# Retention followed by a low-rank mixer MLP on one core: U, V and batch 1 loaded in another order, by other queues, in smaller pieces

## The chip, the cores and the metric

The kernel runs on one core of a Trainium2 chip. The metric is the device time of one execution in microseconds. The kernel before was run seven times: median 248.86 us, from 248.56 to 249.55. One further execution was profiled, and all durations and views below come from it.

## The reference

The first half is a retention layer with a decaying state for each head (4 batches, 8 heads, 768 positions, head size 64). Its output, with the heads side by side, is `x` (4 x 768 x 512). The second half mixes along the sequence with a low-rank product and then runs a two-layer MLP with a residual:

```python
state = gamma[None, :, None, None] * state + np.einsum('bhd,bhe->bhde', k[:, :, t], v[:, :, t])
y[:, :, t] = scale * np.einsum('bhd,bhde->bhe', q[:, :, t], state)
...
h = xt @ U @ V                                   # xt is x with sequence and features exchanged
u = x + h.transpose(0, 2, 1)
ch = np.maximum(u @ w_ch1, 0.0) @ w_ch2
return (u + ch).astype(np.float32)
```

U is 768 x 32, V is 32 x 768, `w_ch1` is 512 x 2048, `w_ch2` is 2048 x 512. Inputs and output are fp32 in HBM; the products are computed in bf16.

## The kernel before, in words

**Stages.** Retention is computed in chunks of 128 positions (six in a batch), as scores within a chunk plus a query against the state that is carried from chunk to chunk. Batch 0 has a path of its own (`cast_early`, `turn_early`, `score_early`, `state_early`, `mix_early`), with two chunks (256 positions) at a time, since nothing else can run yet. Then come the low-rank product of batch 0 (`proj`, the product with V4 at L670, and the turned x that is added to it in PSUM by `x_turn`), and from there on the MLP. The MLP of batch b is a list of pieces (`mlp_pieces`): 16 `up` pieces of 512 columns, 16 of 256 columns, and 24 `down` pieces (six output tiles of 128 rows, four pieces of four matmuls each). A piece of four 512-column matmuls has the cost 0.864 in that list, and a batch has 41.5 in all.

**Weaving.** `weave` puts the retention of batch b+1 between the MLP pieces of batch b. Each step has a mark, which is a share of the list's cost at which it is put into the program: `AT` gives the marks of `score4` and `mix4` of the six chunks, `LR` those of the low-rank part, and `turn_chunk` (two transposes on DVE) and `prep_chunk` (casts on POOL) stand a fixed part of a step before the score. The order is written out by hand; each engine works through its own instructions in that order.

**Who loads what.** SP issues all loads of q, k and v. For batch 0 these are blocks of 256 positions (L158, L154). For batches 1 to 3, `load_whole` (L111) loads k and q of a whole batch by four DMAs each, into tiles of 32-partition stripes, and `feed_more` (L130) loads natural chunks of v (and of k for batches 2 and 3). SP has nothing to wait for after batch 0, so batch 1 follows it at once. POOL issues the weights with a cast to bf16 in the DMA: a quarter of w1 (`load_w1(0)`), U, four copies of V, three more quarters of w1, and later four quarters of w2 (L262, L256, L259, L267). POOL also makes the casts `ki` and `qi` and the scaled `vd` of a chunk (L83, L85), and issues the stores of the output (L427). Each of its DMAs carries one of eight semaphores in turn, and waits until the DMA that had it before has landed.

**Buffers that matter here.** There is one tile each for k and q of a batch (`kin`, `qin`), so batch b+1 can be loaded only once POOL has cast the last chunk of batch b. MLP results go through three PSUM banks (`mlp`). The output tiles `o_sb` have three buffers, so the sum of output tile j+3 on DVE waits until the store of tile j has landed.

Of the kernel before, what the change touches and what calls it, by code (L numbers as in the profile page):

```python
# [9 lines left out]
fp32 = mybir.dt.float32  # L10
# [6 lines left out]
def kernel(  # L17
# [52 lines left out]
    def evac(eng, dst, src):  # L70
        if eng == "A":
            nc.scalar.activation(dst, src, AF.Copy)  # L72
        else:
            nc.vector.tensor_copy(out=dst, in_=src)
# [32 lines left out]
    def load_whole(nm, b):  # L107
        open_in(nm, b)
        src = {"q": q, "k": k}[nm][b]
        for hp in (0, 2, 1, 3):  # L110
# [3 lines left out]
                in_=src[ds(2 * hp, 2)].rearrange("h (c t j) d -> t (h c) (j d)",  # L114
                                                 c=NCK, t=32))

    def feed_more():
        while n_fed[0] < len(feed) and n_held[0] < RING:
            key, src = feed[n_fed[0]]
            if key[0] == "T" and n_cast[key[1] - 1] < 2 * NCK:  # L120
                return
            n_fed[0] += 1
            if key[0] == "T":
                load_whole("k", key[1])
                load_whole("q", key[1])
                continue
            n_held[0] += 1
            t = rin.tile([P, 512], fp32, tag="in", name=f"in_{n_fed[0]}")
            ready[key] = t
            nc.sync.dma_start(out=t.rearrange("p (h d) -> p h d", h=H), in_=src)  # L130
# [2 lines left out]
        n_held[0] -= 1  # L133
        return ready.pop(key)

    for b in range(1, B):
        feed.append((("T", b), None))
        for ci in range(NCK):
            if b > 1:
                feed_natural("k", b, ci)  # L140
            feed_natural("v", b, ci)
    NB = S // 256
    early = {}
# [108 lines left out]
            prep_natural("k", b, ci)  # L252
        prep_natural("v", b, ci)

    def load_u():
        nc.gpsimd.dma_start(out=Ub, in_=moe_U.rearrange("(j p) r -> p j r", p=P))  # L256

    def load_v(c):
        nc.gpsimd.dma_start(out=V4[ds(RK * c, RK)], in_=moe_V)  # L259

    def load_w1(mb):
        nc.gpsimd.dma_start(  # L262
            out=w1b[:, :, ts(mb, 512)],
            in_=moe_w_ch1[:, ts(mb, 512)].rearrange("(c p) n -> p c n", p=P))
# [164 lines left out]
    def mlp_pieces(b):  # L429
        gT = gtp.tile([P, NM, S], bf16, tag="gT", name=f"gT_{b}")  # L430
        pieces = []
        n = [0]

        def up(m, lo, sz):
            def f():
                g_p = bank("mlp")
                for c in range(NCB):
                    nc.tensor.matmul(g_p[:, :sz], w1b[:, c, ts(m, P)],  # L438
                                     uTs[b][:, c, ds(lo, sz)], start=(c == 0),
                                     stop=(c == NCB - 1))  # L440
# [12 lines left out]
        hold = {}  # L453

        def down(j, m0):
            def f():
                if m0 == 0:
                    hold[j] = bank("mlp")
                ch = hold[j]
                for m in range(m0, m0 + 4):  # L460
                    nc.tensor.matmul(ch, gT[:, m, ts(j, P)], w2b[:, m],  # L461
                                     start=(m == 0), stop=(m == NM - 1))
                if m0 == NM - 4:
                    o_sb = outp.tile([P, DM], fp32, tag="o_sb",
                                     name=f"o_{b}_{j}")
                    nc.vector.tensor_tensor(o_sb, ch, us[b][:, j], op=ALU.add)  # L466
                    stores.append((out[b, ts(j, P)], o_sb))
            return f

        for j in range(NCK):  # L470
            for m0 in range(0, NM, 4):
                pieces.append((0.864, down(j, m0)))
        return pieces
# [178 lines left out]
    def proj(js):  # L652
        for j in js:
            for c in range(NCB):
                nc.tensor.matmul(p_p[ds(RK * c, RK), :P], Ub[:, j],  # L655
                                 xs[0][:, j, ts(c, P)], start=(j == 0),
                                 stop=(j == NCK - 1))

    state_early(4)
    for c in range(NCB):  # L660
        x_turn(c, range(2))
    mix_early(2, "DA")
    proj(range(4))
    for c in range(NCB):
        x_turn(c, range(2, NLO))
    proj(range(4, NCK))
    pcs[0] = rmid.tile([P, P], bf16, tag="pc", name="pc_0")
    evac("D", pcs[0], p_p[:, :P])
    for c in (0, 2, 1, 3):
        nc.tensor.matmul(xT(c)[:, :LO], pcs[0][ds(RK * c, RK)],  # L670
                         V4[ds(RK * c, RK), :LO], start=False, stop=True,
                         skip_group_check=True)
# [12 lines left out]
    prep_natural("v", 1, 1)  # L685
    prep_natural("v", 1, 2)
    load_w2(2)
    load_w2(3)

    def at(b0, dc, dm):  # L690
        return [(b0 + dc * ci, b0 + dc * ci + dm) for ci in range(NCK)]

    AT = {1: at(0.36, 0.0625, 0.042), 2: at(0.09, 0.105, 0.05)}
    LR = {1: (0.80, 0.83, 0.88, 0.92), 2: (0.71, 0.75, 0.83, 0.89)}
    for b in range(1, B):
        w = min(b, 2)
        if b > 1:
            marks = [(0.02, part(lr_expand, b - 1, 4, 2)),
                     (0.06, part(lr_turn, b - 1, 4))]
        else:  # L700
            marks = [(0.03, part(lr_expand, 0, 4, 2)), (0.10, part(lr_turn, 0, 4)),
                     (0.16, part(lr_expand, 0, 0, 4))]
        step = AT[w][1][0] - AT[w][0][0]
        for ci in range(NCK):
            s_at, m_at = AT[w][ci]
            marks.append((s_at - 0.6 * step, part(turn_chunk, b, ci)))
            marks.append((s_at, part(score4, b, ci)))
            marks.append((m_at, part(mix4, b, ci)))
# [44 lines left out]
```

## Time and profile before

| what | value |
|---|---|
| median of seven runs | 248.86 us (248.56 to 249.55) |
| the profiled execution: its own time, its span | 249.43 us, 247.5 us |
| busy shares of the span: PE, DVE, ACT, POOL | 88%, 43%, 33%, 37% |
| first MLP matmul of batch 0, of batch 1 | 41.1 us, 97.4 us |
| last matmul starts, last store issued | 241.1 us, 242.5 us |
| moved by DMA in 247.5 us | 34.69 MB, mean 140 GB/s |
| DMA issued by SP (q1), by POOL (q0) | 23.60 MB, 10.73 MB |

The profiled execution took 0.57 us more than the median of the seven runs, and 1.93 us of its time lie outside the span. In the strips with 40 slices a slice is 6.2 us and a digit is a tenth: PE is busy with gaps in the first 45 us and then in nearly every slice to the end. The DMA strip is at 9 from the second slice to the sixteenth, that is to about 100 us, and from then on has holes.

### The profile page before, as it was taken

To read this page: it belongs to the slowest core of one execution; us is meant where nothing else is said; L and a number is where in the kernel's file an instruction comes from. 1 tells how busy PE (TensorE), PEld (TensorE's weight loads), DVE (VectorE), ACT (ScalarE), POOL (GpSimd) and SP (SyncE) were. 2 spreads that over 40 slices of the span, in tenths; PEclk is the share of its full clock that TensorE was granted. 3 is DMA by queue.
4 is the path that set the end of the run, shared out by engine and by line. 5 is a ranking of instruction groups with operands and counts; after the bars stand their busy time and mean duration, and the time that the engine had idled before them with its cause. 6 is when DMAs were issued, how large, how long until landed. Compare 5 with 4: busy or idle time off the path is not lost.

```text
span 247.5 us, 5673 instructions
## 1 busy us (share of the span) xinstructions
PE 217.7 (88%) x2412; PEld 119.9 (48%) x2412; DVE 106.4 (43%) x199; ACT 80.7 (33%) x176; POOL 90.9 (37%) x126
## 2 busy tenths in 40 slices
PE   1686607999999899899999999999999999999990
PEld 1465503447854444445754444457644444674440
DVE  4567104465555352466534525655545242322211
ACT  2474302535733104555641003555420024440000
POOL 2748540893602494851138516810011100001110
PEclk9996755899999999999999999999999999999998
DMA  6999999999799999129999853000012531001221
GB/s 186 290 294 208 226 225 197 201 181 199 157 203 203 217 259 250 43 74 209 211 192 256 213 144 98 16 3 4 0 45 87 128 106 21 3 0 42 86 86 42
DMA packets 63881, 34.69 MB, mean 140 GB/s; under 512 B 39664, under 2 KB 62320, under 8 KB 63856
## 3 DMA queue, kind: packets, MB, share of 16 engines
q1 hardware_dynamic: 56736, 23.60, 47.4%
q0 software_dynamic: 7120, 10.73, 18.3%
q8 instruction: 19, 0.31, 0.6%
q14 instruction: 6, 0.05, 0.1%
HBM read 30.90 MB, written 6.29 MB: 150 GB/s over the span
## 4 chain that ended last, share of the span: by engine, by line
PE 48%; issue 30%; DMA 9%; SPq 5%; POOL 3%; ACT 1%; DVE 1%; POOLq 0%; ACTq 0%
PE mlp L438 22%; PE mlp L461 17%; DMA Ub<-in_moe_U_dram 6%; DMA v<-in_v_dram 3%; SPq L158 3%; POOL out_dram L427 2%; SPq L154 2%; PE r L367 2%; PE r L334 2%; PE st L319 1%; PE r L358 1%; PE r L416 1%; ACT gT L445 1%; PE r L395 1%; PE mlp L296 0%
## 5 line engine op out<-in xcount | busy, mean ns | idle before, releaser
L438 PE MATMUL mlp<-uT,w1b 128*128 128x512 bf16 (+1 forms) x512 | 90.9, 330 | 2.4 <-ACT gT L445 1.2
L461 PE MATMUL mlp<-w2b,gT 128*128 128x512 bf16 x384 | 87.8, 379 | 1.1 <-issue 1.1
L445 ACT ACTIVATE gT<-mlp 128x512 bf16<-128x512 f32 (+1 forms) x88 | 42.7, 490 | 69.7 <-PE mlp L438 68.9
L438 PEld LDWEIGHTS <-w1b 128*128 128x128 bf16 x512 | 48.3, 98 | 35.2 <-issue 5.5
L461 PEld LDWEIGHTS <-gT 128*128 128x128 bf16 x384 | 35.8, 98 | 42.1 <-issue 1.8
L427 POOL DMA_DIRECT2D out_dram<-o x24 | 13.3, 556 | 94.3 <-DVE o L466 94.3
L443 DVE TENSOR_SCALAR gT<-mlp 128x512 bf16<-128x512 f32 (+1 forms) x40 | 22.1, 554 | 33.8 <-PE mlp L438 33.8
L466 DVE TENSOR_TENSOR o<-mlp,u 128x512 f32<-128x512 f32 x24 | 16.6, 690 | 42.8 <-PE mlp L461 42.8
L340 DVE TENSOR_TENSOR a<-r,mask 128x512 bf16<-128x512 f32 x36 | 23.2, 686 | 21.2 <-PE r L334 19.5
L85 POOL TENSOR_TENSOR qi<-qin,gqT 128x512 bf16<-128x512 f32 x18 | 18.8, 1046 | 22.0 <-DMA qin<-in_q_dram 15.1
L85 POOL TENSOR_TENSOR vd<-in,gk 128x512 bf16<-128x512 f32 x18 | 18.7, 1042 | 10.1 <-PE r L367 5.0
L72 ACT ACTIVATE x<-r 128x256 bf16<-128x256 f32 x36 | 11.8, 382 | 25.4 <-PE r L367 25.2
L402 DVE TENSOR_TENSOR u<-r,x 128x512 bf16<-128x512 f32 (+1 forms) x16 | 14.6, 951 | 4.2 <-PE r L395 4.2
L83 POOL CAST ki<-kin 128x512 bf16<-128x512 f32 x18 | 13.6, 766 | 7.6 <-DMA kin<-in_k_dram 5.0
L72 ACT ACTIVATE uT<-r 128x1024 bf16<-128x1024 f32 (+1 forms) x6 | 5.2, 880 | 21.8 <-PE r L670 11.3
L655 PE MATMUL mlp<-x,Ub 128*32 128x128 bf16 x24 | 1.0, 304 | 8.9 <-DMA Ub<-in_moe_U_dram 8.9
L83 POOL CAST kd<-in 128x512 bf16<-128x512 f32 x12 | 7.3, 610 | 1.6 <-POOL qi L85 1.6
L519 PE MATMUL mlp<-ident,kb 128*128 128x128 bf16 x24 | 3.1, 312 | 5.4 <-DVE kb L83 5.4
L284 DVE STREAM_TRANSPOSE kT<-ki 128x256 f32<-128x256 f32 x18 | 7.8, 436 | 0.0
L72 ACT ACTIVATE ns<-st 128x256 bf16<-128x256 f32 x15 | 5.8, 387 | 4.9 <-PE st L319 4.8
L367 PE MATMUL r<-vd,a 128*128 128x64 bf16 x144 | 7.3, 194 | 0.0
L284 DVE STREAM_TRANSPOSE qT<-qi 128x256 f32<-128x256 f32 x18 | 7.3, 404 | 0.0
(74 smaller groups left out, 139.2 us busy)
## 6 DMA issues: line engine op xcount, KB each, us to landing
out_dram<-o POOLq DMA_DIRECT2D x24, 256.0 KB, 2.8
kin<-in_k_dram SPq DMA_DIRECT2D x12, 384.0 KB, 8.1
qin<-in_q_dram SPq DMA_DIRECT2D x12, 384.0 KB, 13.7
in<-in_v_dram SPq DMA_DIRECT2D x18, 256.0 KB, 6.3
in<-in_k_dram SPq DMA_DIRECT2D x12, 256.0 KB, 6.0
w1b<-in_moe_w_ch_dram POOLq DMA_DIRECT2D x4, 512.0 KB, 14.3
w2b<-in_moe_w_ch_dram POOLq DMA_DIRECT2D x4, 512.0 KB, 10.1
kin<-in_k_dram SPq DMA_DIRECT2D x3, 512.0 KB, 6.4
```

The source lines that it names most:

```text
L72: nc.scalar.activation(dst, src, AF.Copy)
L83: e.tensor_copy(out=dst, in_=src)
L85: e.tensor_tensor(dst, src, scale, op=ALU.mult)
L284: nc.vector.transpose(out=dst, in_=src)
L340: nc.vector.tensor_tensor(a[:, ds(4 * g, 4)].rearrange("p (n i) m -> p n i m", n=2), R[g][:, :, :256].rearrange("p n (i m) -> p n i m", i= ...
L402: nc.vector.tensor_tensor(v4(us[b][:, ds(j0, nj), e]), R[g][:, :, :nj * P].rearrange("p c (j e) -> p c j e", j=nj), v4(xs[b][:, ds(j0, nj) ...
L427: nc.gpsimd.dma_start(out=dst, in_=src)
L438: nc.tensor.matmul(g_p[:, :sz], w1b[:, c, ts(m, P)], uTs[b][:, c, ds(lo, sz)], start=(c == 0), stop=(c == NCB - 1))
L443: nc.vector.tensor_relu(gT[:, m, ds(lo, sz)], g_p[:, :sz])
L445: nc.scalar.activation(gT[:, m, ds(lo, sz)], g_p[:, :sz], AF.Relu)
L461: nc.tensor.matmul(ch, gT[:, m, ts(j, P)], w2b[:, m], start=(m == 0), stop=(m == NM - 1))
L466: nc.vector.tensor_tensor(o_sb, ch, us[b][:, j], op=ALU.add)
```

## The change

- **U and V** are loaded in fp32 by SP into ring tiles (`load_uv`: one DMA for U, eight for four copies of V in two column ranges), right behind batch 0, and cast to bf16 by POOL (`cast_uv`, three casts) after the second quarter of w1 is issued. POOL's five DMAs for U and V are gone.
- **Batch 1** is no longer loaded by SP. `load_part(ci)` loads one chunk by POOL: two DMAs each for k and q (four heads, 128 partitions, 1 KB runs) and one for v. POOL's order becomes: w1(0), w1(1), U and V casts, part 0, w1(2), part 1, prep 0, w1(3), part 2, prep 1, part 3, w2(0), prep 2, part 4, w2(1), part 5; then woven prep 3, prep 4, w2(2), prep 5, w2(3). SP's next DMAs after V are those of batch 2.
- **The front of batch 0**: `x_turn` moves behind `mix_early(2)` and between the two parts of `proj`; `state_early(2)` stands ahead of `score_early(2)`; some evictions and casts change engine; two extra matmuls into a spare bank (`fill(2)`) stand between the product with V and the MLP; the four evictions of uT are two on ACT, two on DVE, by halves.
- **The marks** of batch 1: the first score is at 0.17 of the list, the next every 0.075 (before: 0.36, 0.0625), and the low-rank marks begin at 0.66 (before: 0.80). By this, casts of batch 2 are put ahead of the first store of batch 0 on POOL.
- **The last output tile** is computed as 384 and 128 columns; the second part is stored by SP.

```diff
+    def load_part(ci):
+        if ci == 0:
+            open_in("k", 1)
+            open_in("q", 1)
+        for nm, src in (("k", k), ("q", q)):
+            for h in range(2):
+                nc.gpsimd.dma_start(
+                    out=turned_in[nm, 1][:, h, ci],
+                    in_=src[1, ds(h, 4, step=2), ts(ci, P)].rearrange(
+                        "h (t j) d -> h t (j d)", j=4))
+        t = rin.tile([P, 512], fp32, tag="in", name=f"v1_{ci}")
...
+        nc.gpsimd.dma_start(out=t.rearrange("p (h d) -> p h d", h=H),
+                            in_=v[1, :, ts(ci, P)].rearrange("h p d -> p h d"))
...
-    for b in range(1, B):
+    for b in range(2, B):
         feed.append((("T", b), None))
...
-    def load_u():
-        nc.gpsimd.dma_start(out=Ub, in_=moe_U.rearrange("(j p) r -> p j r", p=P))
-
-    def load_v(c):
-        nc.gpsimd.dma_start(out=V4[ds(RK * c, RK)], in_=moe_V)
+    def load_uv():
+        uv["u"] = rin.tile([P, 512], fp32, tag="in", name="uf")
+        nc.sync.dma_start(out=uv["u"][:, :NCK * RK].rearrange("p (j r) -> p j r", j=NCK),
+                          in_=moe_U.rearrange("(j p) r -> p j r", p=P))
+        for lo, sz in ((0, LO), (LO, S - LO)):
+            t = uv[lo] = rin.tile([P, 512], fp32, tag="in", name=f"vf_{lo}")
+            for c in range(NCB):
+                nc.sync.dma_start(out=t[ds(RK * c, RK), :sz], in_=moe_V[:, ds(lo, sz)])
+
+    def cast_uv():
+        cast("P", Ub.rearrange("p j r -> p (j r)"), uv["u"][:, :NCK * RK])
+        for lo, sz in ((0, LO), (LO, S - LO)):
+            cast("P", V4[:, ds(lo, sz)], uv[lo][:, :sz])
...
         for j in range(NCK):
+            if (b, j) == (B - 1, NCK - 1):
+                for n0, nn in ((0, 384), (384, 128)):
+                    for m0 in range(0, NM, 4):
+                        pieces.append((0.864 * nn / DM, down(j, m0, n0, nn)))
+                continue
...
-    turn_early("q", 0, "AD")
+    turn_early("q", 0)
...
-    turn_early("q", 1, "AD")
+    turn_early("q", 1, "D")
...
-    cast_early("q", 2, ("P", 5, 3), ("D", 0, 5))
+    cast_early("q", 2, ("P", 4, 4), ("D", 0, 4))
...
+    state_early(2)
+    score_early(2)
+    load_uv()
     load_w1(0)
-    score_early(2)
-    state_early(2)
     cast_early("v", 2, ("P", 0, 4), ("P", 4, 4))
-    load_u()
-    for c in range(NCB):
-        load_v(c)
-    for mb in range(1, 4):
-        load_w1(mb)
+    load_w1(1)
+    cast_uv()
...
     state_early(4)
+    mix_early(2, "DA")
+    spare = bank("mlp")
+    proj(range(4))
     for c in range(NCB):
         x_turn(c, range(2))
-    mix_early(2, "DA")
-    proj(range(4))
-    for c in range(NCB):
-        x_turn(c, range(2, NLO))
     proj(range(4, NCK))
     pcs[0] = rmid.tile([P, P], bf16, tag="pc", name="pc_0")
     evac("D", pcs[0], p_p[:, :P])
+    for c in range(NCB):
+        x_turn(c, range(2, NLO))
...
+    fill(2)
     for c in range(NCB):
-        evac("AD"[c % 2], uTs[0][:, c, :LO], xT(c)[:, :LO])
+        evac("AD"[c // 2], uTs[0][:, c, :LO], xT(c)[:, :LO])
     late_consts()
     n_cast[0] = 2 * NCK
     feed_more()
-    for ci in range(3):
-        prep_turned("k", 1, ci)
-    for ci in range(3):
-        prep_turned("q", 1, ci)
-    prep_natural("v", 1, 0)
+    load_part(0)
+    load_w1(2)
+    load_part(1)
+    prep_chunk(1, 0)
+    load_w1(3)
+    load_part(2)
+    prep_chunk(1, 1)
+    load_part(3)
     load_w2(0)
+    prep_chunk(1, 2)
+    load_part(4)
     load_w2(1)
-    prep_natural("v", 1, 1)
-    prep_natural("v", 1, 2)
-    load_w2(2)
-    load_w2(3)
+    load_part(5)
...
-    AT = {1: at(0.36, 0.0625, 0.042), 2: at(0.09, 0.105, 0.05)}
-    LR = {1: (0.80, 0.83, 0.88, 0.92), 2: (0.71, 0.75, 0.83, 0.89)}
+    AT = {1: at(0.17, 0.075, 0.045), 2: at(0.09, 0.105, 0.05)}
+    LR = {1: (0.66, 0.70, 0.76, 0.82), 2: (0.71, 0.75, 0.83, 0.89)}
...
                 marks.append((s_at - 0.55 * step, part(prep_chunk, b, ci + 3)))
+                if b == 1 and ci:
+                    marks.append((s_at - 0.5 * step, part(load_w2, ci + 1)))
```

More of the change, by code (lines that the diff above doesn't have):

```diff
@@ L115, in load_whole @@
                                                  c=NCK, t=32))
+    def load_part(ci):
[9 more added lines that the diff above has]
+        t = rin.tile([P, 512], fp32, tag="in", name=f"v1_{ci}")
+        n_held[0] += 1
+        ready["v", 1, ci] = t
+        nc.gpsimd.dma_start(out=t.rearrange("p (h d) -> p h d", h=H),
+                            in_=v[1, :, ts(ci, P)].rearrange("h p d -> p h d"))
     def feed_more():
@@ L134, in take @@
         return ready.pop(key)
-    for b in range(1, B):
+    for b in range(2, B):
         feed.append((("T", b), None))
         for ci in range(NCK):
-            if b > 1:
-                feed_natural("k", b, ci)
+            feed_natural("k", b, ci)
             feed_natural("v", b, ci)
@@ L253, in prep_chunk @@
         prep_natural("v", b, ci)
-    def load_u():
-        nc.gpsimd.dma_start(out=Ub, in_=moe_U.rearrange("(j p) r -> p j r", p=P))
-    def load_v(c):
-        nc.gpsimd.dma_start(out=V4[ds(RK * c, RK)], in_=moe_V)
+    uv = {}
+    def load_uv():
[10 more added lines that the diff above has]
+            cast("P", V4[:, ds(lo, sz)], uv[lo][:, :sz])
     def load_w1(mb):
@@ L453, in mlp_pieces, with down @@
         hold = {}
-        def down(j, m0):
+        def down(j, m0, n0=0, nn=DM):
             def f():
                 if m0 == 0:
-                    hold[j] = bank("mlp")
-                ch = hold[j]
+                    hold[j, n0] = bank("mlp")
+                ch = hold[j, n0]
                 for m in range(m0, m0 + 4):
-                    nc.tensor.matmul(ch, gT[:, m, ts(j, P)], w2b[:, m],
+                    nc.tensor.matmul(ch[:, :nn], gT[:, m, ts(j, P)],
+                                     w2b[:, m, ds(n0, nn)],
                                      start=(m == 0), stop=(m == NM - 1))
@@ L464, in f @@
                     o_sb = outp.tile([P, DM], fp32, tag="o_sb",
-                                     name=f"o_{b}_{j}")
-                    nc.vector.tensor_tensor(o_sb, ch, us[b][:, j], op=ALU.add)
-                    stores.append((out[b, ts(j, P)], o_sb))
+                                     name=f"o_{b}_{j}_{n0}")[:, :nn]
+                    n = ds(n0, nn)
+                    nc.vector.tensor_tensor(o_sb, ch[:, :nn], us[b][:, j, n],
+                                            op=ALU.add)
+                    if n0:
+                        nc.sync.dma_start(out=out[b, ts(j, P), n], in_=o_sb)
+                    else:
+                        stores.append((out[b, ts(j, P), n], o_sb))
             return f
         for j in range(NCK):
+            if (b, j) == (B - 1, NCK - 1):
[3 more added lines that the diff above has]
+                continue
             for m0 in range(0, NM, 4):
@@ L657, in proj, with fill @@
                                  stop=(j == NCK - 1))
+    def fill(n):
+        for _ in range(n):
+            nc.tensor.matmul(spare, ident, w1b[:, 0, :512], start=True, stop=True)
     state_early(4)
+    mix_early(2, "DA")
+    spare = bank("mlp")
+    proj(range(4))
     for c in range(NCB):
         x_turn(c, range(2))
-    mix_early(2, "DA")
-    proj(range(4))
-    for c in range(NCB):
-        x_turn(c, range(2, NLO))
     proj(range(4, NCK))
```

## The prediction

> **What bounds the kernel now.** I read the chain of waits first, then PE's own waits, then POOL, SP and the DMA share where PE is late. The chain in order of time (start, length, what), around the start of the MLP:
>
> ```profile
> 23.59 13.75 DMA Ub<-in_moe_U_dram
> 37.34 0.04 issue
> 37.39 0.62 PE mlp L655 x16
> ...
> 39.71 0.72 PE r L670 x4
> 40.43 0.59 ACT uT L72
> ...
> 41.79 3.10 PE mlp L438 x7
> 44.89 0.22 PE r L395 x8
> 45.11 2.70 PE mlp L438 x12
> ```
>
> The end of retention waits for U, 13.75 us in flight. Then the MLP starts at 41.79, and its first two pieces take 3.10 us where a piece takes 0.87. PE's waits (us, times, longest):
>
> ```profile
> PE mlp L655 <- DMA Ub<-in_moe_U_dram: 8.9, 1, 8.9
> ```
>
> and the strips of granted clock and DMA:
>
> ```profile
> PEclk9996755899999999999999999999999999999998
> DMA  6999999999799999129999853000012531001221
> ```
>
> 8.9 us is the largest gap of PE in the run. After 45 us PE waits for little: 41.5 us of pieces, 3.1 of low-rank steps and 7.6 of retention from an effective start of 43.2 (41.79 and 1.4 lost to the half clock) make 95.4, and batch 1's MLP starts at 97.55. So PE bounds from 45 us on, with some 2.2 us of stalls; DMA is full to 100 us, but ahead of need. The third reading is of the timelines of POOL and SP where batch 2 begins to load, and of the issues of w1 (us to landing):
>
> ```profile
> 75.00 0.61 POOL L427 DMA_DIRECT2D out_dram<-o  x1 [7.22 <-DVE o L466]
> 75.62 0.77 POOL L83 CAST ki<-kin 128x512 bf16<-128x512 f32 x1
> 83.48 1.04 POOL L85 TENSOR_TENSOR qi<-qin,gqT 128x512 bf16<-128x512 f32 x1 [7.08 <-DMA qin<-in_q_dram]
> ```
>
> ```profile
> 64.33 1.87 SPq L111 DMA_DIRECT2D kin<-in_k_dram  x4
> 66.30 4.87 SPq L111 DMA_DIRECT2D qin<-in_q_dram  x4
> ```
>
> ```profile
> w1b<-in_moe_w_ch_dram POOLq DMA_DIRECT2D x4, 512.0 KB, 14.3
> ```
>
> SP starts batch 2 at 64.33, when POOL has cast the last k chunk of batch 1. Its k and q (3.1 MB) move until 80.6 at 0.205 MB/us (DMA by windows of 2 us: 0.40 to 0.41 MB in q1). The store issued at 75.00 gets no packet before 80 and lands after 9.2 us; later stores take 2.3 to 5.3. The first quarter of w1, issued at 20.22, gets none before 27 and lands after 13.8. Both times what SP had issued earlier (1.1 to 1.4 MB) moved first.
>
> **What the Trainium skill says.** "DMA: Bandwidth & Descriptors", section on queues, rings and completion order: each DMA engine goes round between its queues packet by packet. The trace disagrees in these two places: 5 and 6 us without one packet for the later queue. I take the measurement. "TensorE: Matmul & The Clock Gate", part 1: about 3.4 us idle halve the clock, and about 3.4 us of work restore it. The trace agrees: granted clock 0.50 from 37 to 44 us, and full at 45.
>
> **The change, part by part.**
>
> *Start of the MLP.* SP is done with batch 0's issues at 14.8, so U is issued there instead of at 23.59, with 4.72 MB ahead of it. At 0.29 MB/us (2 to 12 us: 2.83 MB) that is gone by 18.6; U lands near 21, the last V near 24.5. Batch 1 no longer sits between. POOL: the scaled v of batch 0 by 21.9, w1(1) to 22.7, three casts (0.35, 0.75, 0.4 by the 0.77 of a 512-column cast) to 24.9. `mix_early(2)` ended at 28.48 behind 0.83 us of `x_turn`, now at 27.6. PE is busy from 23.5 on, so the clock, full at 27.3 before too, stays full, and the L655, L613, L670 rows (0.62, 0.97, 0.40, 0.97, 0.61) count half: 1.8 us, with 0.3 for small gaps. `fill(2)` (0.43) lies beside the four evictions of uT, 1.3 us on two engines. MLP start 27.6 + 2.1 + 1.3 = 31.0: **10.8 us earlier, and 1.4 of cold clock saved**. Other engine swaps and the new place of `state_early(2)` I cost at nothing: POOL's v casts cover them; without that cover 0.5 us.
>
> *POOL's new queue.* From 24.9 it must do, in order: 6 parts; w1(2), w1(3); w2(0) to w2(2); preps 0 to 4; the k cast of 5. A DMA issue costs 0.50 (V, 32 rows), 0.54 (store, 128), 0.80 (w1, 512), 0.90 (U, 768). So a part is 4 x 0.52 + 1.0 = 3.1 (bounds 2.6 and 3.5). A prep is 0.69 + 0.99 + 0.98 = 2.66 by distances between starts. 18.6 + 1.6 + 2.3 + 13.3 + 0.7 = 36.5: **POOL casts the last k chunk at 61.4**, 2.9 us before it did. The waits on the DMA eight before mostly end earlier: a part moves in some 3.2 us (0.52 MB of k, q at 0.29; v in 1.4), a weight quarter in 3.1 (0.17 MB/us at 53 to 62 us). w1(2) lands near 35 (needed 38.9), w1(3) near 41 (needed 44).
>
> *Chunk 3.* Parts 4 and 5 stand ahead of its casts, so its q is ready at 61.4 - 5.1 = 56.3 and turned at 56.7. PE is at its score (0.395 x 41.5 = 16.4 us of pieces, 1.0 low-rank, 3.7 retention) at 31.0 + 21.1 = 52.1. **4.6 us of new wait**, with DVE's in-order queue held behind the transposes, its ReLUs too.
>
> *w2(3).* From there to the fourth piece of the first output tile are 7.0 us of pieces and 3.3 of retention: 67, or 68 with half a clock period lost. But w2(3) is issued after q and v of prep 5, at 63.4, and SP begins k of batch 2 (1.57 MB) at 61.4. By the store it would take 9.2 + 1.5 for its larger size = 10.7, by w1(0) 13.8: it lands at 74.1 to 77.2, I take 75.7. **7.7 us of new wait**, and 1 of clock.
>
> *To the end.* 18.1 of pieces, 1.7 low-rank, 0.6 retention and that clock lead to 97.1, against 97.55: 0.45 left of 12.2. Stores of batch 0 now stand behind preps of batch 2 on POOL. The fourth load of batch 2's chunks landed by 87 (64.33 + 22.7), now 61.4 + 22.7 + 3.1 for w2(3) = 87.2; the first store goes out at 89, the third by 93 and lands by 98; the sum that waits for it and the next u end at 100, where PE needs them at 101.4: hidden, by 1.4 us. Last tile: before, 0.69 sum, 0.3 and 2.3 to landing; now 0.25, 0.3 and about 2.1, with the 384 columns out earlier (16 matmuls of 128 columns at 0.056 = 0.9): 0.6 less, bounds 0 and 1.2. Batches 2 and 3 keep their order. Sum: -0.45 - 0.6 = **-1.05 on 249.43**; the median lies 0.57 lower, so 247.8.
>
> **The rivals.**
>
> *Slower: w2(3) lands behind q of batch 2 too.* SP starts q at 63.3, a tenth before w2(3) is issued. The whole 1.57 MB ahead would add 7.6 us (landing 83.5); half of it, interleaved as at 27 to 31 us, lands at 79.5 and gives 251.6. It decides from a landing past 76.8. For it: w1(0) had all of k ahead of it and shared with q. Against: the store waited no longer than its backlog. Parts that cost POOL 3.5 do the same (2.4 later).
>
> *Faster: the queues share.* If w2(3) gets its turns at once, it lands near 72. Then the store chain binds: it is 2.1 us ahead of before, so -2.7: 246.2; with parts at 2.6 on POOL all shifts by 3 us, to 243.5. For it: the skill's rule. Against: both cases above.
>
> *It does not do what it says:* V's last copies wait for U, and semaphores return only in turn. If V lands past 29, the product with V waits, and each us is lost from a start that POOL's queue hides anyway: within 1 us of 248.9.
>
> **Numbers.** 0.2% (0.5 us) is about what can be told from no change here. Forecast (landing 74.1 to 77.2: 246.3 to 249.3): 0.45, of it 0.34 faster, 0.08 same, 0.03 slower. Slower rival 0.34 (0.02 same). Faster rival 0.18. Last 0.03 (0.01 same, 0.02 slower). Sum 0.52, 0.11, 0.37. Range 243.6 to 252.2: it leaves out landings past 80 and parts cheaper than 2.6.
>
> **What would show it.** Right: first MLP matmul near 31, no wait for U; clock at 1 there; PE idle near 52 to 57 with DVE on transposes that wait for POOL; PE idle for w2(3) near 68 to 76; SP's k of batch 2 starting near 61; batch 1's MLP near 97. Wrong: no wait for w2(3), POOL with idle time between 25 and 61, or a first MLP matmul after 35.

## The result, and the profile after

The changed kernel takes **256.66 us** (median of 12 runs, 254.52 to 258.03) against 249.06 for the kernel before beside it: ratio 1.0301, 95% interval 1.028 to 1.0323. The forecast was 247.8 in a range of 243.6 to 252.2, so neither its sign nor its range held. The profiled execution took 258.03 us with a span of 256.3, against 249.43 and 247.5; it was the slowest of the twelve, 1.4 us above their median.

The front does what was forecast, and 1.8 us more. There is no wait for U any more, the first MLP matmul is at 29.21 us, and its clock is full. The chain of waits (start, length, what) now runs through POOL and a transfer of w2 where it ran through U:

```profile
28.04 0.70 POOL kin L123
...
70.14 0.93 POOL vd L85
71.07 13.32 DMA w2b<-in_moe_w_ch_dram
...
84.43 3.57 PE mlp L486 x8
```

From 28 to 71 us this chain is POOL's queue, with two transfers in it (a k part and a v part) that POOL waited for; it ends in w2(3), issued at 71.07 and landed at 84.39. PE's own waits (us, times, longest) name two places:

```profile
PE mlp L321 <- DVE kT L309: 8.0, 3, 6.2
PE mlp L486 <- DMA w2b<-in_moe_w_ch_dram: 7.3, 1, 7.3
...
PE mlp L463 <- DMA w1b<-in_moe_w_ch_dram: 1.7, 1, 1.7
```

6.2 us is the wait for the transposed k of chunk 3 (DVE transposes it once POOL has cast it), which ends at 63.54; 7.3 is w2(3). The strips, 6.4 us a slice, show both as a fall of the granted clock (the 5 and the next 5 of PEclk):

```profile
PEclk9997999996597599999999999999999999999998
DMA  7998799899599999714999965300002343001112
```

POOL's timeline (start, length, engine, line, operation, tiles, count) at the first part, and at the end of batch 1:

```profile
26.83 0.40 POOL L83 CAST V<-vf 128x256 bf16<-128x256 f32 x1 [2.21 <-DMA vf<-in_moe_V_dram]
27.32 1.43 POOL L123 DMA_DIRECT2D kin<-in_k_dram  x2
28.73 1.34 POOL L123 DMA_DIRECT2D qin<-in_q_dram  x2
30.07 0.93 POOL L130 DMA_DIRECT2D v<-in_v_dram  x1
...
68.40 0.77 POOL L83 CAST ki<-kin 128x512 bf16<-128x512 f32 x1
69.08 1.05 POOL L85 TENSOR_TENSOR qi<-qin,gqT 128x512 bf16<-128x512 f32 x1
70.08 1.04 POOL L85 TENSOR_TENSOR vd<-v,gk 128x512 bf16<-128x512 f32 x1
71.07 0.80 POOL L292 DMA_DIRECT2D w2b<-in_moe_w_ch_dram  x1
```

A part costs POOL 1.43 + 1.34 + 0.93 = 3.70 us where 3.1 was reckoned. POOL hardly waited for earlier parts to land (busy us and mean ns of one, then idle us before these issues and what ended it):

```profile
L123 POOL DMA_DIRECT2D qin<-in_q_dram x12 | 8.1, 678 | 1.5 <-DMA kin<-in_k_dram 1.5
```

By windows it was busy 35.4 of the 37 us from 28 to 65, while the DMA engines too were nearly full (0.91 to 1.02); then they ran dry, with POOL casting and w2(3) not yet issued (start and end, PE busy, PEld, DVE, ACT, POOL, then granted clock, DMA share and GB/s):

```profile
65.00:67.00 2.00, 2.00 (x18) 1.38 (x11) 1.30 (x3) 0.38 (x1) 2.00 (x3) 0.50 0.58 131
67.00:69.00 2.00, 2.00 (x11) 1.44 (x10) 1.09 (x3) 0.69 (x2) 2.00 (x3) 0.50 0.08 27
69.00:71.00 2.00, 2.00 (x50) 1.37 (x49) 0.42 (x1) 1.02 (x5) 2.00 (x3) 0.85 0.84 128
```

And the SP queue, where batch 2 begins 1.9 us ahead of the issue of w2(3):

```profile
69.19 1.95 SPq L111 DMA_DIRECT2D kin<-in_k_dram  x4
71.44 8.48 SPq L111 DMA_DIRECT2D qin<-in_q_dram  x4
```

Batch 1's MLP starts at 107.67, 10.3 us later than in the kernel before, though batch 0's began 11.9 us earlier. The windows around the end of the second wait, with the same columns:

```profile
85.00:87.00 2.00, 2.00 (x7) 0.66 (x5) 0.66 (x1) 0.00 (x0) 0.00 (x0) 0.50 1.15 208
...
89.00:91.00 2.00, 2.00 (x8) 0.83 (x7) 0.00 (x0) 0.36 (x2) 0.00 (x0) 0.73 1.35 180
```

PE resumes at 84.43 and is at half speed until about 90.1 (0.73 in the last window): 5.7 us at half, so 2.8 us lost.

Six of the ten executions of parts_by_sp_32 below, the profiled one among them, and one of the four of front_w2_ahead ran slower than the others of the same kernel; medians and ratios leave them out, but the trace of parts_by_sp_32 is from such a run.

### The profile page after: what moved, and what is told of

Same layout as the page of the kernel before. It is cut to its first block, busy times and chain, and to the rows that moved or that the text cites. A ratio compares the mean times of both kernels' runs of the same rounds, so it can differ in the third digit from the quotient of the medians.

```text
span 256.3 us, 5736 instructions
## 1 busy us (share of the span) xinstructions
PE 221.0 (86%) x2430; PEld 121.3 (47%) x2430; DVE 107.5 (42%) x199; ACT 80.6 (31%) x175; POOL 111.6 (44%) x154
## 4 chain that ended last, share of the span: by engine, by line
PE 34%; issue 30%; DMA 15%; POOL 14%; DVE 2%; SPq 2%; ACT 1%; POOLq 0%; ACTq 0%; DVEq 0%
PE mlp L486 12%; PE mlp L463 12%; DMA w2b<-in_moe_w_ch_dram 5%; DMA kin<-in_k_dram 4%; POOL out_dram L452 2%; POOL vd L85 2%; DMA v<-in_v_dram 2%; DMA qin<-in_q_dram 2%; POOL qin L123 2%; POOL qi L85 2%; SPq L435 2%; DMA uT<-u 1%; POOL kin L123 1%; POOL ki L83 1%; PE mlp L555 1%
## 5 line engine op out<-in xcount | busy, mean ns | idle before, releaser
L486 PE MATMUL mlp<-w2b,gT 128*128 128x512 bf16 (+2 forms) x400 | 89.2, 378 | 7.5 <-DMA w2b<-in_moe_w_ch_dram 7.3
L463 PE MATMUL mlp<-uT,w1b 128*128 128x512 bf16 (+1 forms) x512 | 92.0, 332 | 3.1 <-DMA w1b<-in_moe_w_ch_dram 1.7
L486 PEld LDWEIGHTS <-gT 128*128 128x128 bf16 x400 | 37.7, 99 | 49.6 <-issue 10.2
L493 DVE TENSOR_TENSOR o<-mlp,u 128x512 f32<-128x512 f32 (+2 forms) x25 | 16.8, 670 | 56.9 <-PE mlp L486 50.1
L468 DVE TENSOR_SCALAR gT<-mlp 128x512 bf16<-128x512 f32 (+1 forms) x40 | 22.1, 551 | 32.9 <-PE mlp L463 32.9
L72 ACT ACTIVATE x<-r 128x256 bf16<-128x256 f32 x36 | 11.8, 382 | 30.5 <-PE r L392 30.3
L85 POOL TENSOR_TENSOR vd<-in,gk 128x512 bf16<-128x512 f32 x12 | 12.5, 1039 | 6.4 <-PE r L392 3.5
L321 PE MATMUL mlp<-ident,kT 128*128 128x128 bf16 x20 | 2.2, 237 | 8.0 <-DVE kT L309 8.0
L359 PE MATMUL r<-qT,kT 32*128 32x128 bf16 x288 | 7.4, 221 | 1.5 <-DVE qT L309 1.5
L123 POOL DMA_DIRECT2D qin<-in_q_dram x12 | 8.1, 678 | 1.5 <-DMA kin<-in_k_dram 1.5
L123 POOL DMA_DIRECT2D kin<-in_k_dram x12 | 8.6, 717 | 0.2 <-issue 0.2
L582 DVE TENSOR_TENSOR a<-r,mask 128x1024 bf16<-128x1024 f32 x6 | 7.1, 1216 | 3.9 <-PE r L577 3.9
```

Source lines behind the costliest of these rows:

```text
L85: e.tensor_tensor(dst, src, scale, op=ALU.mult)
L123: nc.gpsimd.dma_start(out=turned_in[nm, 1][:, h, ci], in_=src[1, ds(h, 4, step=2), ts(ci, P)].rearrange("h (t j) d -> h t (j d)", j=4))
L463: nc.tensor.matmul(g_p[:, :sz], w1b[:, c, ts(m, P)], uTs[b][:, c, ds(lo, sz)], start=(c == 0), stop=(c == NCB - 1))
L486: nc.tensor.matmul(ch[:, :nn], gT[:, m, ts(j, P)], w2b[:, m, ds(n0, nn)], start=(m == 0), stop=(m == NM - 1))
L493: nc.vector.tensor_tensor(o_sb, ch[:, :nn], us[b][:, j, n], op=ALU.add)
```

## The experiments

All runs in one table, ratios to the kernel before on the same chip; the number behind a name is that of the experiment below. The last three columns are the first MLP matmul of batch 0 and of batch 1, and the issue of w2(3), each from that kernel's profiled execution.

| kernel | median us | ratio (95%) | MLP 0 | MLP 1 | w2(3) |
|---|---|---|---|---|---|
| before | 249.06 | 1 | 41.1 | 97.4 | 52.4 |
| after | 256.66 | 1.0301 (1.028 to 1.0323) | 29.2 | 107.7 | 71.1 |
| w2_before_prep5 (1) | 254.2 | 1.0191 (1.0167 to 1.0216) | 28.9 | 102.0 | 68.1 |
| w2_and_stores_before (2) | 252.25 | 1.0127 (1.0057 to 1.0196) | 30.0 | 95.5 | 67.4 |
| marks_of_before (3) | 259.74 | 1.0416 (1.0399 to 1.0434) | 30.3 | 109.5 | 71.2 |
| parts_by_sp (4) | 268.36 | 1.0759 (1.0738 to 1.078) | 28.8 | 117.8 | 82.3 |
| tail_split_on_before (7) | 248.04 | 0.9958 (0.9939 to 0.9977) | 40.9 | 97.7 | 52.3 |
| front_no_hold (8) | 242.32 | 0.9729 (0.9677 to 0.9782) | 29.2 | 91.4 | 55.4 |
| front_and_hold (8) | 245.28 | 0.9854 (0.9805 to 0.9904) | 28.8 | 93.6 | 59.8 |
| front_w2_ahead (8) | 242.62 | 0.9696 (0.9632 to 0.9759) | 29.3 | 92.4 | 57.3 |
| v_by_sp (5) | 253.77 | 1.0202 (1.0145 to 1.0258) | 28.7 | 104.1 | 68.3 |
| pool_dose (5) | 258.57 | 1.0366 (1.0333 to 1.0399) | 29.5 | 108.9 | 72.8 |
| cast3_ahead_of_parts (6) | 258.81 | 1.0364 (1.0328 to 1.0401) | 29.5 | 109.3 | 72.7 |
| parts_by_sp_32 (4) | 252.6 | 1.0108 (1.0068 to 1.0148) | 29.8 | 107.0 | 72.8 |
| parts_front_order (9) | 254.79 | 1.0196 (1.0159 to 1.0233) | 29.1 | 104.6 | 69.5 |
| whole_new_order (9) | 249.30 | 0.9968 (0.9934 to 1.0001) | 29.6 | 100.2 | 64.8 |

Several kernels scatter by 1 to 2 us from run to run, and most were run four times, so differences between them below 1 us say nothing here. The tail alone was run 20 times.

**1. Is it w2(3)?** The two quarters of w2 that stand behind preps 4 and 5 on POOL are put ahead of them.

```diff
-                    marks.append((s_at - 0.5 * step, part(load_w2, ci + 1)))
+                    marks.append((s_at - 0.6 * step, part(load_w2, ci + 1)))
```

> Edit: the marks of the third and fourth quarter of w2 are a little earlier, so that POOL issues w2(2) ahead of prep 4 and w2(3) ahead of prep 5, thus before SP may start k of batch 2. Theory A (POOL's queue is late, and w2(3) then queues in the DMA behind k of batch 2; stores of batch 0 stand behind casts of batch 2): PE's wait of 7.3 us for w2 and about 1.8 of half clock after it go, but the first store is issued at 98 or 99 us all the same, behind the casts that wait for batch 2, and the sums that wait for store buffers hold PE: 253 to 254, with PE idle near 100 to 105 instead. Theory B (w2(3) alone is the loss): 247 to 249. Theory C (the early marks of batch 1 are the loss): 256 to 257, as the changed kernel.

254.2 us, as theory A said. The wait for w2 is gone, and the cover is gone with it. PE's waits:

```profile
PE mlp L321 <- DVE kT L309: 6.5, 1, 6.5
...
PE mlp L463 <- DVE o L493: 4.8, 1, 4.8
```

The 4.8 us, at 101.96, are the chain of stores: the first store of batch 0 goes out at 97.09, behind casts of batch 2. In the changed kernel the same chain is as late (first store 97.83), but PE is later still. So w2(3) is not the loss by itself: what stands beside it in POOL's queue is as late.

**2. And the stores?** On top of that, the preps of batch 2 are put at later marks.

```diff
-                marks.append((m_at + 0.05, part(prep_chunk, b + 1, ci - 3)))
+                late = (0.64, 0.70, 0.765)[ci - 3] if b == 1 else m_at + 0.05
+                marks.append((late, part(prep_chunk, b + 1, ci - 3)))
```

> Edit: as the last, and the first three casts of batch 2 get the marks 0.64, 0.70, 0.765, as in the kernel before, so that the first stores of batch 0 stand ahead of them on POOL. Theory A: the whole of the wait for w2 is kept as a gain, 247 to 248.5, and the first store is issued right after its sum, near 79 us. Theory B: as the last kernel, within 0.5 us. Theory C: 256 to 257.

252.25 us: 2 us, not the 6 of theory A. The first store now goes at 77.22, but the second only at 93.45, since it stands behind a cast that waits for q of batch 2. Both repairs together take back about 4.4 of the 7.6 us. Batch 1's MLP now starts at 95.5, 1.9 us ahead of the kernel before, but PE then waits 3.2 us at L441 for the low-rank sum on DVE, and from there to the end this kernel takes some 4 us more than the kernel before; how much of that is due to the late second store was not tried apart.

**3. The marks.** The changed kernel with `AT` and `LR` of the kernel before.

```diff
-    AT = {1: at(0.17, 0.075, 0.045), 2: at(0.09, 0.105, 0.05)}
-    LR = {1: (0.66, 0.70, 0.76, 0.82), 2: (0.71, 0.75, 0.83, 0.89)}
+    AT = {1: at(0.36, 0.0625, 0.042), 2: at(0.09, 0.105, 0.05)}
+    LR = {1: (0.80, 0.83, 0.88, 0.92), 2: (0.71, 0.75, 0.83, 0.89)}
```

> Edit: the marks of batch 1 (AT and LR) are those of the kernel before, all loads and POOL's order to w2(3) stay. Theory A: POOL casts the last k at the same 69 us and w2(3) lands at 84 as it did; the waits for chunks 2 and 3 become part of a longer wait for w2(3); 254 to 257. Theory C: the waits go with the marks, 247 to 250.

259.74 us, above both theories: slower, so with loads in parts the early marks are not the fault. With later retention PE runs out of pieces sooner and waits 16.6 us for w2 in three waits; k of batch 2 still starts at 69.29. POOL's queue hardly moved.

**4. Parts by SP instead of POOL.** First the same transfers:

```diff
-                nc.gpsimd.dma_start(
+                nc.sync.dma_start(
                     out=turned_in[nm, 1][:, h, ci],
...
-        nc.gpsimd.dma_start(out=t.rearrange("p (h d) -> p h d", h=H),
+        nc.sync.dma_start(out=t.rearrange("p (h d) -> p h d", h=H),
```

> Edit: the 30 DMAs of load_part are issued by SP instead of POOL, in the same order; nothing else. Theory A: POOL loses 23.8 us of issuing ahead of the last casts of batch 1; PE's waits for chunks 1 to 3 (9.5 us) and for w2(3) (7.3) go, with 3 us of half clock; SP's k of batch 2 starts near 50 instead of 69. Some of it comes back where w1(2) and w1(3) queue behind the parts: 238 to 243. Theory B: only the wait for w2(3) goes, 247 to 249. Theory C: not under 252.

268.36 us: theory C, and 16 us beyond its bound of 252. Then with k and q of a chunk in four transfers of 32 partitions each, v by SP as in the last:

```diff
+            for hp in (0, 2, 1, 3):
+                nc.sync.dma_start(
+                    out=turned_in[nm, 1][ds(32 * hp, 32), :, ci],
+                    in_=src[1, ds(2 * hp, 2), ts(ci, P)].rearrange(
+                        "h (t j) d -> t h (j d)", j=4))
...
```

> The changed kernel with batch 1 still loaded chunk by chunk, but by SP, k and q in four transfers of 32 partitions a chunk instead of two whose source has four heads as outer dimension, v in one. Theory A (POOL's issues are what costs, and the earlier version by SP was slow for the form of its transfers): POOL is 18 us of issues lighter, chunks come at 4 to 5 us each from 22 us on, no wait of PE over 3 us before the w2 of batch 0, 240 to 246 us. Rival B (loading batch 1 in chunks beside w1 is slow by itself, on either queue): 253 us or more. Rival C (SP's in-order queue, at some 0.5 us an issue and 54 issues, is as long as POOL's was): 247 to 252 us.

252.6 us, ratio 1.0108: between rival C (to 252) and rival B (from 253). The two differ only in the form, and so the number, of the transfers of k and q. Windows of 25 to 75 us, first the four-head form:

```profile
25.00:75.00 50.00, 36.17 (x433) 20.35 (x429) 21.21 (x45) 19.46 (x45) 17.09 (x20) 0.86 0.67 138
```

then the 32-partition form:

```profile
25.00:75.00 50.00, 39.05 (x552) 23.59 (x556) 24.40 (x52) 21.83 (x51) 21.90 (x25) 0.91 0.91 183
```

The DMA engines are busy 0.67 against 0.91 of the time, at 138 against 183 GB/s. Issued by POOL, in the changed kernel, the four-head form has 0.93 and 173 GB/s in these 50 us. The Trainium skill, "DMA: Bandwidth & Descriptors", section "Why a DMA increments its semaphore by 16 and not by 1", says that a transfer is spread over the largest number of engines up to 16 that divides the slowest dimension of both sides: here four (four heads), and from SP always the lowest-numbered four; 16 for a transfer of 32 partitions. The two runs are in line with it; which engines were busy, no view here shows. Even the better form doesn't rescue the change: v and q of a chunk land late, POOL's casts wait for them (3.7 to 4.8 us for v of chunks 1 to 3), and w2(3), behind those casts in POOL's order, is again issued at 72.8.

**5. How stiff is POOL's queue?** Six v issues taken off it, and four casts put on it:

```diff
-        nc.gpsimd.dma_start(out=t.rearrange("p (h d) -> p h d", h=H),
+        nc.sync.dma_start(out=t.rearrange("p (h d) -> p h d", h=H),
```

```diff
...
+    for _ in range(4):
+        nc.gpsimd.tensor_copy(out=four(dose), in_=jmat[:, None, :].to_broadcast([P, 4, P]))
     load_part(4)
```

> The changed kernel, with the six v parts of batch 1 issued by SP instead of POOL (0.93 us each on POOL in the changed kernel's trace, 5.6 us in all; a v part's transfer keeps its form). Theory A (POOL's in-order queue of issues and casts sets the time): POOL's last k cast of batch 1 moves from 68.4 to about 63, SP's k of batch 2 and the issue of the last quarter of w2 with it, batch 1's MLP starts near 102.5 instead of 107.7: 251 to 252.5 us. Rival B (arrival of bytes sets it, POOL only waits): POOL waits for kin and qin grow by as much, 256 to 257 us. Rival C (SP's in-order queue is slow for such parts): v arrives late, over 258 us.

> The changed kernel with four casts of a 128x512 tile on POOL, whose output nobody reads, ahead of the issues of the fifth part of batch 1 (four times 0.75 us, by the cast row of the trace). Theory A (POOL's queue between 25 and 70 us sets the time): everything behind them on POOL moves by 3.0 us, k of batch 2 and w2(3) too: 2.5 to 3.2 us longer than the changed kernel, 259.2 to 260. Rival B (POOL has slack there, its waits for the arrival of parts take it up): under 1 us longer, 256.5 to 257.7.

Both lie between their theories. Taking 5.6 us off POOL moved its last k cast of batch 1 from 68.40 to 65.63 and w2(3) by 2.8, and the time fell by 2.5 to 2.9 us (by ratio, by median). The four casts took 2.64 us, not 3.0:

```profile
53.20 2.64 POOL L730 CAST dose<-ramp 128x512 bf16<-128x512 f32 x4
...
70.12 0.77 POOL L83 CAST ki<-kin 128x512 bf16<-128x512 f32 x1
...
72.80 0.80 POOL L293 DMA_DIRECT2D w2b<-in_moe_w_ch_dram  x1
```

They moved the last cast and w2(3) by 1.7 us, and the time rose by 1.6 to 1.9. So the time follows POOL's queue, as the issue of w2(3) shows its lateness, about one for one; by the intervals the first is 1.0 to 4.0 us and the second 0.6 to 2.6, so the rate is not known closely. The issue of w2(3) follows about half to two thirds of the work taken from POOL or given to it. The rest is taken up by POOL's waits for the landing of earlier parts, which shrink or grow: in the run with v on SP one issue of q waits 3.07 us for a k part that it had not waited for.

**6. Or its order?** The casts of chunk 3 ahead of parts 4 and 5.

```diff
+    prep_chunk(1, 3)
     load_part(4)
     load_w2(1)
...
-                marks.append((s_at - 0.55 * step, part(prep_chunk, b, ci + 3)))
+                if b > 1 or ci:
+                    marks.append((s_at - 0.55 * step, part(prep_chunk, b, ci + 3)))
```

> The changed kernel with the three casts of chunk 3 of batch 1 moved on POOL ahead of the issues of parts 4 and 5 (and of w2(1)), nothing added or removed. Theory A (the sum of POOL's work sets it, its order only chooses where PE stands): the 6.2 us wait for chunk 3 shrinks to under 1.5, the last k cast stays within 2 us of 68.4, w2(3) is issued no sooner, and PE waits at w2 or at chunks 4 and 5 instead: 255 to 259 us. Rival B (parts ahead of casts is the fault): 250 to 252 us.

258.81 us, theory A: about 1.6 us slower than the changed kernel by ratio. PE's waits:

```profile
PE mlp L486 <- DMA w2b<-in_moe_w_ch_dram: 11.5, 2, 11.0
...
PE mlp L321 <- DVE kT L309: 0.9, 1, 0.9
```

The wait for chunk 3 went from 6.2 to 0.9 us, and the one for w2(3), issued 1.6 us later, from 7.3 to 11.0. The chunk 3 wait cost next to nothing by itself: it was time that PE would have spent waiting for w2(3).

**7. The tail alone**, on the kernel before (the edit of the last output tile in the change).

> The kernel before with one part of the change alone: the last output tile in 384 and 128 columns, the 128 stored by SP. Theory A (the term of the forecast): the sum that ends the last tile falls from 0.69 us to about 0.29, the last landing from 2.3 to about 2.1: 0.6 us less, so 248.4 where before is 249.0, nothing else moved. Rival B (the second store and the extra 16 short matmuls cost what the shorter sum saves): within 0.3 us of before.

0.9958 (0.9939 to 0.9977), which is 1.05 us with 0.6 to 1.5: theory A, at the lower bound of the interval. DVE's last sums:

```profile
241.02 0.56 DVE L468 TENSOR_TENSOR o<-mlp,u 128x384 f32<-128x384 f32 x1 [1.91 <-PE mlp L461]
241.91 0.29 DVE L468 TENSOR_TENSOR o<-mlp,u 128x128 f32<-128x128 f32 x1 [0.34 <-PE mlp L461]
```

**8. The first half alone.** U and V ahead on SP, the front of batch 0 and the tail as changed; batch 1 loaded whole by SP, marks, casts and w2 as in the kernel before.

```diff
-    load_part(0)
     load_w1(2)
-    load_part(1)
-    prep_chunk(1, 0)
     load_w1(3)
-    load_part(2)
-    prep_chunk(1, 1)
-    load_part(3)
+    for ci in range(3):
+        prep_turned("k", 1, ci)
+    for ci in range(3):
+        prep_turned("q", 1, ci)
+    prep_natural("v", 1, 0)
     load_w2(0)
-    prep_chunk(1, 2)
-    load_part(4)
     load_w2(1)
-    load_part(5)
+    prep_natural("v", 1, 1)
+    prep_natural("v", 1, 2)
+    load_w2(2)
+    load_w2(3)
...
```

> The first half of the change alone, without holding batch 1: U and V ahead on SP and cast on POOL, the moved transposes of x, the split last tile; k and q of batch 1 are loaded whole by SP and v by SP, as in the kernel before, and the marks, the issues of w2 and the casts stand as in the kernel before. Theory A (the loss of the changed kernel comes from POOL's loads of batch 1 and what stands behind them): the first quarter of w1 again moves behind k of batch 1 and lands near 34, the MLP starts there (29.2 in the changed kernel, 41.8 before), the w2 waits of the changed kernel are absent: 243 to 246 us. Rival B (whatever is loaded, weights and batch 1 cannot arrive sooner, so an earlier MLP only waits later): waits of PE for w1 or w2 of together 6 us or more appear, 247.5 to 250 us.

The same with batch 1 held back, and with the last two quarters of w1 issued earlier:

```diff
+    load_w1(2)
+    load_w1(3)
+    nc.gpsimd.tensor_copy(out=kin0[:, NB - 1, 0, :1], in_=w1b[:, 0, :1])
...
```

> As the kernel with the first half alone, but batch 1 is held until the first quarter of w1 has landed: all four quarters of w1 are issued by POOL by about 27 us, and a one-column copy on POOL that reads that quarter and writes the last column of batch 0's k tile makes SP's load of k of batch 1 wait for it. k, q and v of batch 1 go by SP in one piece each as before, marks, w2 and casts as before. Theory A: MLP start near 29.2 to 30 as in the changed kernel, k of batch 1 lands near 40, q near 48, a wait for q at chunk 0 of up to 4 us, w2 behind it: 240 to 244 us. Rival B (the arrival of bytes binds): PE waits for q and w2 of batch 1 give the 12 us back, 247 to 250 us.

**242.32 us without holding, just below its theory A; 245.28 with it, between its two theories.** The first half gains nearly 7 us, of which the tail is 1; what each of the edits to the front brings was not tried apart. Theory A missed one thing to the good: the MLP starts at 29.16, not 34. SP reaches k of batch 1 only at 22.1, behind its nine issues for U and V, and by then w1(0), issued at 19.95, is ahead of it. Rival B's sign is there as well: PE waits 5.3 us for w2 and 1.2 for w1, 6.5 together, and of the 11.9 us by which batch 0's MLP starts sooner batch 1's MLP keeps 6.0. So the arrival of bytes takes back about half of what the front wins, but not all of it. Holding batch 1 for w1 was not needed, and as built here it costs 3 us: the wait for q of chunk 0 is 6.1 us longer, those for w2 are 3.4 shorter. PE's waits with holding:

```profile
PE r L344 <- DVE qT L294: 7.2, 1, 7.2
...
PE mlp L471 <- DMA w2b<-in_moe_w_ch_dram: 1.9, 2, 1.3
```

and without:

```profile
PE mlp L471 <- DMA w2b<-in_moe_w_ch_dram: 5.3, 4, 2.2
...
PE r L344 <- DVE qT L294: 1.1, 1, 1.1
```

The 5.3 us in four led to one more try, w2(0) and w2(1) ahead of the q casts:

```diff
+    load_w2(0)
+    load_w2(1)
     for ci in range(3):
         prep_turned("q", 1, ci)
     prep_natural("v", 1, 0)
-    load_w2(0)
-    load_w2(1)
```

> The front half alone without holding (242.3 us), with the first two quarters of w2 issued ahead of the q casts of batch 1 on POOL, where POOL stood idle from 40 to 47 us. Theory A (PE waits 5.3 us in four for w2, issued at 51 us; an earlier issue fills them): w2 waits under 2 us, the wait for q of chunk 0 up by about 1, 239 to 241 us. Rival B (DMA is full there, so w2 only takes what q and v then miss): 242 to 244 us, with q or v of chunk 0 late by 2 to 4 us.

242.62 us (0.9696, 0.9632 to 0.9759), not to be told from 242.32. The waits are those of rival B: the ones for w2 go, and 3.2 us of waiting for v of batch 1 come in their place.

**9. A table of two by two.** Loads whole by SP or in parts by POOL, in the order and marks of the first half alone or in those of the changed kernel.

```diff
+    load_w1(2)
+    load_w1(3)
+    for ci in range(NCK):
+        load_part(ci)
     for ci in range(3):
         prep_turned("k", 1, ci)
...
```

> The first half alone without holding, but batch 1 loaded in the changed kernel's parts by POOL, all 30 issues in a row behind the four quarters of w1; casts, w2 and marks in the order of the kernel before. Theory A (POOL's issues of the parts are the cost): 6 parts of 3.7 us end near 51, the q cast that chunk 0 needs comes near 54 instead of 47, w2 is issued near 59 instead of 51: 250 to 254 us. Rival B (the new order and the marks cost it, the parts little): 242 to 246 us.

```diff
     def load_part(ci):
         if ci == 0:
-            open_in("k", 1)
-            open_in("q", 1)
+            load_whole("k", 1)
+            load_whole("q", 1)
...
+        nc.sync.dma_start(out=t.rearrange("p (h d) -> p h d", h=H),
+                          in_=v[1, :, ts(ci, P)].rearrange("h p d -> p h d"))
```

> The changed kernel with k and q of batch 1 loaded whole and v by SP, as in the kernel before; w1(2), w1(3), w2 stay between the casts of POOL, and the early marks stay. Theory A (POOL's issues of the parts are the cost): 242 to 246 us. Rival B (the order is the cost: q of chunk 0 lands near 47, so w1(3), behind its cast on POOL, is issued near 50 and lands near 58 where PE needs it at 44): a wait for q near 36 and one for w1 near 48, 252 to 260 us.

| us | order and marks of the first half | of the changed kernel |
|---|---|---|
| whole, by SP | 242.3 | 249.3 |
| parts, by POOL | 254.8 | 256.7 |

The parts cost 12.5 us in one order and 7.4 in the other; the order costs 7.0 with whole loads and 1.9 with parts (by the ratios, which compare on the same chip: 11.6, 8.3, 6.0 and 2.6). The first try lies just above its theory A, the second between its theories. So both are at fault, and they hide each other: each makes POOL's last casts and w2 late (w2(3) is issued at 55.4 with neither, 64.8 with the order, 69.5 with the parts, 71.1 with both), and PE's waits for the two fall together. With parts in the front's order POOL's issues fill 28.72 to 59.14, of which some 22 us are issues and 8 are waits for earlier transfers. PE's waits there:

```profile
PE mlp L321 <- DVE kT L309: 14.6, 1, 14.6
```

and the windows show what the DMA engines did once POOL had turned to casting:

```profile
63.00:64.00 1.00, 1.00 (x20) 0.62 (x9) 0.61 (x2) 0.00 (x0) 1.00 (x2) 0.50 0.00 0
...
65.00:66.00 1.00, 1.00 (x6) 0.73 (x5) 0.78 (x3) 0.00 (x0) 1.00 (x3) 0.50 0.00 0
```

Nothing moved for 3 us, with POOL busy all of it and w2 not issued before 65.16. It is not the bytes that bind there, it is the queue that has to ask for them. With whole loads in the new order PE waits 8.5 us up to 48.89, since q of a whole batch lands near 46 and the early marks ask for chunk 0 near 40: these marks need parts, and the parts are what POOL has no time for. Two things were not tried: the marks and POOL's order apart with whole loads, and parts by POOL in fewer issues. How much of the 12.5 us comes from standing all parts in a row ahead of the first cast is open too.

## Why the prediction was wrong

What the forecast described is what happened: w2(3), last in POOL's order, went behind k of batch 2, and PE waited for it. The step that failed is the sum for POOL's new queue, which came out 7.7 us short; two smaller terms were short as well.

**The front: right, and better.** Forecast 31.0 with a full clock; 29.21 with a full clock. `mix_early(2)` ended on PE at 25.85, where 27.6 was reckoned; from there to the MLP were 3.4 us, as forecast. The engine swaps and the new place of `state_early(2)`, which the forecast "cost at nothing", were thus worth 1.8 us: of PE's waits from 18 to 24 us, 0.92, 1.47 and 0.85 in the kernel before, 0.20, 0.24 and 0.68 are left. Which swap did it was not tried.

**"A part is 4 x 0.52 + 1.0 = 3.1 (bounds 2.6 and 3.5)": mis-sized.** A k or q issue was priced at 0.52, between a V copy (0.50) and a store (0.54). It took 0.68 to 0.72 us, that of v 0.93; with no waits a part is 3.70, above the upper bound. With their waits the six parts cost 23.75 us instead of 18.6: 5.15 us.

**"Three casts ... to 24.9": mis-sized by the wait.** The last cast of V waited 2.21 us for V to land, so part 0 began at 27.32: 2.4 us. The text reckoned V's landing at 24.5 but only charged a late V to PE, not to POOL's queue behind it. SP's eight issues of V ran from 15.88 to 22.15; whether they held it back was not tried.

**"POOL casts the last k chunk at 61.4": 69.2**, by these two and 0.2 for the rest. So w2(3) was issued at 71.07 instead of 63.4: 7.7 us, the largest part of the miss. The runs with a lighter and with a heavier queue show that POOL's lateness moves the end, about one for one (experiment 5).

**w2(3) behind k of batch 2: right.** Forecast 12.3 us from issue to landing, measured 13.3: 1.0 us, within the forecast's 10.7 to 13.8. The slower rival had the right place (it decides past a landing of 76.8), but not its main reason: q of batch 2 can have added no more than this 1.0 us, POOL's lateness added 7.7. Its last sentence, that parts at 3.5 do the same, names the cause; the forecast gave it no weight of its own.

**"1 of clock": mis-sized.** Half speed lasted 5.7 us after this wait, so 2.8 us were lost. The forecast read the kernel before as agreeing with 3.4 us of work for the way back, but there PE was at work again at 37.39 and the clock at half until about 44.7 (0.65 from 44 to 45): 7.3 us, with pauses of PE of up to 0.7. That row already spoke for a larger loss. From the landing of w2(3) to batch 1's MLP were 23.3 us, forecast 21.4: 1.9.

7.7 + 1.0 + 1.9 = 10.6: forecast start of batch 1's MLP 97.1, measured 107.67. The other steps did not add to it. The waits at chunk 1, chunk 2 and w1(3), which the forecast left out, fall ahead of the wait for w2(3) and are absorbed by it, as the wait for chunk 3 is (experiment 6). That the two waits themselves came near the forecast (6.2 for 4.6 us, 7.3 for 7.7) is luck: both ends of each had moved, that for w2(3) from 68 and 75.7 to 77.1 and 84.4.

**"Hidden, by 1.4 us": true as it happened, wrong in its numbers.** The first store was forecast at 89 and went at 97.83; PE was later still. With w2 mended the stores are the next to bind (experiments 1 and 2).

**The tail: 0.6 forecast, 1.05 measured (0.6 to 1.5).** From batch 1's MLP to the end of the span the changed kernel is 1.5 us shorter than the kernel before; the kernel with the tail alone is 1.0 shorter there, and the other 0.5 I did not trace. The miss closes on the profiled executions: 10.6 - 0.9 = 9.7, and 258.03 is 9.65 above the 248.38 that was reckoned.

In sum the arithmetic had 12.2 us to win and 11.8 to lose, and drew a likeliest value from a balance whose terms were each uncertain by 3 us or more, all through one queue. The forecast's bounds for a part were taken from two small neighbours; a load of the same form would have been needed.

## What to carry to other kernels

Count the engine that issues a transfer as a resource: thirty issues of 0.7 to 0.9 us, with the casts between them, made POOL the bound, to the point that the DMA engines ran dry ahead of the last quarter of w2 (busy 0.08 from 67 to 69 us), and whatever comes last in such a queue (here a quarter of w2) carries its whole lateness. Here the loads of batch 1 did best on the queue that had nothing else to do, in few large transfers. Before holding a transfer back for another one, see whether it would overtake it at all: here the order of issue had already settled that, and the first half of the change alone, without holding, is, with the try that puts w2 ahead, the fastest here at 242.32 us (0.9729, 0.9677 to 0.9782).

## What the hardware showed that I had not expected

- The clock came back late. After both long waits of the changed kernel PE ran at 0.50 for 5.7 us (84.43 to 90.1) and 6.1 us (63.54 to 69.6). The Trainium skill, "TensorE: Matmul & The Clock Gate", part 1, says about 3.4 us of work restore it, and that the window runs freely; here it took 1.7 and 1.8 times that, and a wait of 6 to 7 us cost nearly 3 us more than itself (an estimate: half of the time at half speed). It also fell sooner than I had reckoned: 2.0 and 2.7 us after PE stopped (57.37, 77.14), and 2.6 in the kernel before (28.48).
- Issuing from POOL costs by form. 0.50 us for a V copy of 32 partitions in the kernel before, 0.54 for a store, 0.68 to 0.72 for 128 runs of 1 KB from four heads, 0.80 for a quarter of a weight, 0.93 for v, 1024 runs of 256 bytes.
- The same transfer issued by SP took its place in SP's queue for 1.2 to 1.6 us (median) in the four-head form and 0.43 to 0.47 in the 32-partition form, with half the bytes in each of the latter.
